# Second matmul in four 32-column array tiles where scores, pooling or weights share the session; denominators in other slots

## The chip, the cores and the metric

One core of a Trainium2 chip. The metric is the device time of one execution in microseconds (us), lower is better. The kernel before takes 597.37 us (median of 3 runs, 596.58 to 597.43).

## The reference, cut to what matters

```python
def mab(q, kv):                       # attention; C = 128, scale = 1/sqrt(C)
    a = softmax(scale * (q @ kv.T))
    return a @ kv
h = mab(inducing, x)                  # 32 inducing rows against 12480 rows of x, for 4 batches
y = mab(x, h)                         # 12480 rows of x against the 32 rows of h
hid = y @ w_in                        # 128 -> 2048
out = (max(hid, 0) + alpha * min(hid, 0)) @ w_out      # 2048 -> 128
```

The kernel never forms `y`. It multiplies `h` into `w_in` once for each batch (`hW`), so that the first large matmul of a group of 512 rows contracts over 32 rows alone; it writes the activation as relu plus a linear part; and it divides by the softmax denominator at the very end.

## The kernel before

The work of a group of 512 rows of x is cut into four *sessions* (`j` = 0 to 3), 391 in all. A session fills four PSUM banks (a fill is four matmuls of 32x128 weights, one in each 32-row tile of the array), has ScalarE (ACT) and VectorE (DVE) relu them into `gt`, and then does the 16 second matmuls of the session before it.

```python
def fill(st, g, j):                                   # cut
    for r in range(4):
        ps = bank()                                   # ring of 6 PSUM banks
        mm(ps[:, ...], st.hW[32*r : 32*r+32, j*cp + i, :], rep[32*r : 32*r+32, :t])
    ...                                               # ACT or DVE: gt[:, r] = relu(bank), by a plan

def mm2(st, g, j, gt):                                # cut: a whole group, pp = 128, nb = 4
    for r in range(4):
        for k in range(nb):
            mm(acc[:pp, k, :], gt[:, r, k0 : k0 + pp], W1[:, c, :], ...)

for b, g, j in fills:
    gt = fill(states[b], g, j)
    for fn, _ in tasks.pop((b * NG + g, j), []):
        fn()                                          # the tasks of this session
    if prev is not None:
        mm2(*prev)
    prev = (states[b], g, j, gt)
```

All else is a *task*, put into a session between its fill and its second matmuls:

```python
# scores: four matmuls with 32 columns of weights, each into its own 32 partitions of one bank
for q in range(NQ):
    mm(ps[32*q : 32*q+32, :], st.hT, st.xT[:, s, q, :])         # second scores (b_scores)
    mm(ps[32*q : 32*q+32, :], IT[:], st.xT[:, u, q, :])         # first scores of the next batch (a_scores)
# pooling (a_accum): 16 matmuls of the same form, 128 wide; weights (h_weights): four, 512 wide
# denominators (b_den): four matmuls over all 128 columns, then a reciprocal on DVE
at(g,     b_scores, 3, (320, "A", 490));   at(g + 2, b_den,   3, (130, "D", 250))
at(k,     a_load)                              # x of the next batch, 512 KB by DMA
at(k + 3, a_xpose)                             # its transpose, by DMA
at(k + 5, a_scores, 0, (320, "A", 680));   at(k + 8, a_accum, 3, (240, "D", 220))
at(K,     h_den,    3, (250, "D", 500));   at(K + 1, h_transpose, 1, ...)   # K: five groups before the end
```

The last argument tells a planner, which divides the relus between ACT and DVE, what a task costs on TensorE and on the engine that empties its bank.

The softmax here doesn't subtract the row's maximum and nothing guards it: scores larger than these inputs give would overflow.

## Time and profile before

| | before |
|---|---|
| span of the profiled run | 597.2 us |
| TensorE matmul busy | 582.9 us, 98% |
| DVE, ACT busy | 87%, 85% |
| plain session (294 of them) | 1.327 us |
| session with scores alone | 1.656 us |
| session with linear part and scores; with pooling as well | 1.872; 2.096 us |

Session times are mine, from the trace: from the first fill matmul of one session to that of the next; medians.

The page of the kernel before, busy times (time, share of the span, number of instructions) and granted clock in tenths by slice of the span:

```profile
PE 582.9 (98%) x9186; PEld 435.0 (73%) x9186; DVE 518.6 (87%) x878; ACT 507.1 (85%) x994; POOL 84.9 (14%) x170
...
PEclk9999999999999999999999999999999999999999
...
q8 instruction: 72, 1.18, 0.9%
```

The last line is the DMA queue that brings instructions: 72 packets, 1.18 MB. That is 16 KB a packet. TensorE's 18,400 instructions (loads, matmuls and 29 that wait, signal or drain) over 72 packets make 256 instructions a packet, so I read each packet as a *page* of 256 TensorE instructions.

The timeline of TensorE before, one session with scores (start, duration, what, count):

```profile
82.56 0.38 PE L94 MATMUL ring_85<-rep,hW 32*128 32x512 bf16 x1
...
82.89 0.40 PE L94 MATMUL ring_83<-xT,IT 128*32 128x512 bf16 x4
83.22 1.07 PE L94 MATMUL acc_87<-W_168,gt 128*128 128x128 bf16 x16
84.22 0.38 PE L94 MATMUL ring_84<-rep,hW 32*128 32x512 bf16 x1
```

Read the starts, since durations overlap: the second matmuls' 1.07 us end after the next fill has begun. Fill to scores takes 0.33 us, scores to second matmuls 0.33 us, second matmuls to the next fill 1.00 us. The work in these is 0.216, 0.216 and 16 x 0.056 = 0.90 us (0.216 us is what passes in this trace from the last fill of a session, at 80.475, to its linear part, at 80.691, where the tiling stays). So each change of the array's tiling (32 rows, then 32 columns, then whole) leaves about 0.105 us empty.

What a narrow second matmul would cost could be read off the pooling task, which has its form (128x32 weights, 128 wide):

```profile
81.23 0.40 PE L94 MATMUL ring_84<-xn,e1T 128*32 128x128 bf16 x16
81.56 0.23 PE L94 MATMUL acc_87<-W_168,gt 128*128 128x128 bf16 x1
```

In the trace its 16 matmuls start in groups of four at 81.232, 81.288, 81.344 and 81.400: four at once every 56 ns.

### The profile page before, as it was taken

The page shows a single profiled execution, that of the slowest core. Times are in us where ns is not written, and L with a number is a line of the kernel's source. Part 1 is how long each engine was busy: PE and PEld are TensorE (multiplying, and loading weights), DVE is VectorE, ACT ScalarE, POOL GpSimd, SP SyncE. Part 2 cuts the span into 40 slices and gives each one's busy share as a digit, 9 for nine tenths or more (in the row PEclk, how much of TensorE's full clock was granted, in tenths as well). Part 3 has the DMA queues.
Part 4 walks back from the last instruction along what each step waited for, and adds up shares of the span by engine and source line. Part 5 has one row for each costly group of instructions (what it writes and reads, how often), then busy time and mean ns, then how long its engine had stood idle before and what let it go on. Part 6 is the DMA issues. An engine that isn't in the chain of part 4 may idle for free.

```text
span 597.2 us, 21700 instructions
## 1 busy us (share of the span) xinstructions
PE 582.9 (98%) x9186; PEld 435.0 (73%) x9186; DVE 518.6 (87%) x878; ACT 507.1 (85%) x994; POOL 84.9 (14%) x170
## 2 busy tenths in 40 slices
PE   4999999999999999999999999999999999999997
PEld 3677777777777777677777777777777777777775
DVE  2588899889889998899998989988988898998995
ACT  3588888898889888888888988889888889989886
POOL 6331111010111111101011111101011101101100
PEclk9999999999999999999999999999999999999999
DMA  9644799862237669983134478986212221221211
GB/s 197 161 93 103 162 161 176 172 105 85 68 87 147 134 141 173 166 154 112 40 99 120 101 162 157 173 177 103 86 68 80 80 98 57 83 97 56 93 46 61
DMA packets 79009, 69.18 MB, mean 116 GB/s; under 512 B 53200, under 2 KB 68448, under 8 KB 78912
## 3 DMA queue, kind: packets, MB, share of 16 engines
q0 software_dynamic: 12720, 39.30, 26.4%
q1 hardware_dynamic: 66048, 27.97, 24.2%
q8 instruction: 72, 1.18, 0.9%
q10 hardware_dynamic: 144, 0.52, 0.3%
q14 instruction: 25, 0.20, 0.1%
HBM read 39.94 MB, written 28.62 MB: 115 GB/s over the span
## 4 chain that ended last, share of the span: by engine, by line
PE 58%; ACT 0%; DVE 0%; issue 0%
PE acc_88 L94 21%; PE acc_87 L94 21%; PE ring_85 L94 3%; PE ring_83 L94 3%; PE ring_84 L94 3%; PE ring_82 L94 3%; PE ring_81 L94 3%; PE ring_86 L94 3%; ACT gt L405 0%; DVE gt L407 0%; DVE ob L456 0%
## 5 line engine op out<-in xcount | busy, mean ns | idle before, releaser
L94 PEld LDWEIGHTS <-gt 128*128 128x128 bf16 x6272 | 352.4, 98 | 78.9 <-issue 75.9
L94 PE MATMUL acc_87<-W_168,gt 128*128 128x128 bf16 (+1 forms) x3136 | 209.0, 220 | 0.0
L94 PE MATMUL acc_88<-W_168,gt 128*128 128x128 bf16 (+1 forms) x3136 | 208.8, 220 | 0.0
L465 POOL DMA_DIRECT2D out_dram<-ob x99 | 53.7, 542 | 492.8 <-DVE ob L456 422.3
L405 ACT ACTIVATE gt<-ring_83 128x512 bf16<-128x512 f32 (+1 forms) x160 | 95.5, 597 | 10.9 <-ACT gt L405 5.4
L405 ACT ACTIVATE gt<-ring_81 128x512 bf16<-128x512 f32 (+1 forms) x159 | 95.0, 597 | 11.2 <-PE ring_84 L94 5.6
L94 PE MATMUL ring_82<-rep,hW 32*128 32x512 bf16 (+1 forms) x270 | 101.6, 379 | 0.0
L94 PE MATMUL ring_83<-rep,hW 32*128 32x512 bf16 (+1 forms) x270 | 101.1, 378 | 0.0
L94 PE MATMUL ring_85<-rep,hW 32*128 32x512 bf16 (+1 forms) x267 | 100.4, 379 | 0.3 <-ACT gt L405 0.3
L94 PE MATMUL ring_84<-rep,hW 32*128 32x512 bf16 (+1 forms) x266 | 99.6, 378 | 0.8 <-DVE gt L407 0.8
L94 PE MATMUL ring_86<-rep,hW 32*128 32x512 bf16 (+1 forms) x264 | 99.3, 379 | 0.0
L94 PE MATMUL ring_81<-rep,hW 32*128 32x512 bf16 (+1 forms) x263 | 98.9, 379 | 0.0
L405 ACT ACTIVATE gt<-ring_84 128x512 bf16<-128x512 f32 x147 | 88.2, 600 | 12.0 <-ACT gt L405 5.4
L405 ACT ACTIVATE gt<-ring_85 128x512 bf16<-128x512 f32 (+1 forms) x147 | 87.7, 596 | 11.8 <-PE ring_82 L94 5.3
L405 ACT ACTIVATE gt<-ring_86 128x512 bf16<-128x512 f32 (+1 forms) x143 | 85.6, 599 | 12.3 <-ACT gt L405 5.9
L405 ACT ACTIVATE gt<-ring_82 128x512 bf16<-128x512 f32 (+1 forms) x142 | 84.9, 598 | 12.1 <-PE ring_85 L94 4.4
L407 DVE TENSOR_SCALAR gt<-ring_82 128x512 bf16<-128x512 f32 (+1 forms) x123 | 84.2, 684 | 8.5 <-PE ring_84 L94 4.1
L407 DVE TENSOR_SCALAR gt<-ring_86 128x512 bf16<-128x512 f32 (+1 forms) x116 | 79.4, 684 | 12.9 <-PE ring_82 L94 8.4
L407 DVE TENSOR_SCALAR gt<-ring_84 128x512 bf16<-128x512 f32 (+1 forms) x113 | 77.1, 682 | 9.3 <-PE ring_85 L94 3.8
L407 DVE TENSOR_SCALAR gt<-ring_85 128x512 bf16<-128x512 f32 x115 | 78.9, 686 | 7.1 <-PE ring_81 L94 2.5
L407 DVE TENSOR_SCALAR gt<-ring_83 128x512 bf16<-128x512 f32 x104 | 71.4, 687 | 9.4 <-PE ring_85 L94 4.4
L407 DVE TENSOR_SCALAR gt<-ring_81 128x512 bf16<-128x512 f32 x99 | 68.0, 687 | 6.8 <-PE ring_82 L94 2.3
(321 smaller groups left out, 372.1 us busy)
## 6 DMA issues: line engine op xcount, KB each, us to landing
out_dram<-ob POOLq DMA_DIRECT2D x96, 256.0 KB, 2.8
rep<-e2d SPq DMA_DIRECT2D x92, 128.0 KB, 3.0
xn<-in_x_dram POOLq DMA_DIRECT2D x18, 512.0 KB, 6.2
xn<-in_x_dram POOLq DMA_DIRECT2D x10, 256.0 KB, 8.9
w_out_f<-in_moe_w_out_dram POOLq DMA_DIRECT2D x1, 1024.0 KB, 13.9
xs<-in_x_dram ACTq DMA_DIRECT2D x1, 512.0 KB, 4.0
xs<-in_x_dram SPq DMA_DIRECT2D x1, 512.0 KB, 5.0
w_in_b<-in_moe_w_in_dram POOLq DMA_DIRECT2D x1, 512.0 KB, 11.9
```

The lines of the kernel that those rows point to most:

```text
L94: return pin(nc.tensor.matmul(o, lhsT, rhs, start=start, stop=stop, **kw))
L405: pin(nc.scalar.activation(out=gt[:, r, :w], in_=ps[:, :w], func=RELU))
L407: pin(nc.vector.tensor_relu(gt[:, r, :w], ps[:, :w]))
L465: pin((nc.sync if last_one else nc.gpsimd).dma_start(out=dst, in_=ob[:pp, :nb, :]))
```

## The change

The intent: in a session with scores, pooling or weights, do the second matmuls in the same tiling (four 32-column tiles), so that the session changes tiling twice and not three times. Denominators, which use the whole array, leave the pooling sessions for the second session of a group.

```diff
-    def mm2(st, g, j, gt):
+    def mm2(st, g, j, gt, narrow=False):
+        step = 32 if narrow else pp
...
-                    mm(acc[:pp, k, :], gt[:, r, k0 : k0 + pp], W1[:, c, :], ...)
+                    for t in range(0, pp, step):
+                        mm(acc[t : t + step, k, :], gt[:, r, k0 + t : k0 + t + step], W1[:, c, :], ...)
...
-            at(g, b_scores, 3, (320, "A", 490))
-            at(g + 2, b_den, 3, (130, "D", 250))
+            at(g, b_scores, 3, (216, "A", 490), True)
+            at(g + 2, b_den, 1, (130, "D", 250))
-                at(k + 5, a_scores, 0, (320, "A", 680))
-                at(k + 8, a_accum, 3, (240, "D", 220))
+                at(k + 5, a_scores, 0, (216, "A", 680), True)
+                at(k + 8, a_accum, 3, (225, "D", 220), True)
-            at(K, h_den, 3, (250, "D", 500))
+            at(K + 1, h_den, 0, (250, "D", 500))
-            at(K + 1, h_weights, 3, (320, "D", 600))
+            at(K + 1, h_weights, 3, (216, "D", 600), True)
# the session's second matmuls are narrow if its last task with a cost has True
```

(Lambdas are left out of the `at` lines, here and in the edits below, which are shortened.) 60 sessions become narrow, each with 48 more weight loads and 48 more matmuls.

More of the change, by code (lines that the diff above doesn't have):

```diff
@@ L419, in mm2 @@
                     k0 = (i * nb + k) * pp
-                    mm(
-                        acc[:pp, k, :], gt[:, r, k0 : k0 + pp], W1[:, c, :],
-                        start=(j == 0 and r == 0 and i == 0 and k == 0 and not begun),
-                        stop=False, skip_group_check=True,
-                    )
+                    for t in range(0, pp, step):
+                        mm(
+                            acc[t : t + step, k, :], gt[:, r, k0 + t : k0 + t + step], W1[:, c, :],
+                            start=(j == 0 and r == 0 and i == 0 and k == 0 and not begun),
+                            stop=False, skip_group_check=True,
+                        )
         if j == NJ // cp - 1 and st.b * NG + g > 0:
@@ L605, with at @@
     tasks = {}
-    def at(slot, fn, j=1, cost=None):
-        tasks.setdefault((slot, j), []).append((fn, cost))
+    def at(slot, fn, j=1, cost=None, narrow=False):
+        tasks.setdefault((slot, j), []).append((fn, cost, narrow))
     def late_finish():
@@ L629 @@
             g = base + s * NQ - 4
-            at(g, lambda b=b, s=s: b_scores(states[b], s), 3, (320, "A", 490))
+            at(g, lambda b=b, s=s: b_scores(states[b], s), 3, (216, "A", 490), True)
             at(g + 1, lambda b=b, s=s: b_rep(states[b], s), 3)
-            at(g + 2, lambda b=b, s=s: b_den(states[b], s), 3, (130, "D", 250))
+            at(g + 2, lambda b=b, s=s: b_den(states[b], s), 1, (130, "D", 250))
         if b + 1 < B:
@@ L643 @@
                 at(k + 3, lambda n=n, u=u: a_xpose(states[n], u))
-                at(k + 5, lambda n=n, u=u: a_scores(states[n], u), 0, (320, "A", 680))
-                at(k + 8, lambda n=n, u=u: a_accum(states[n], u), 3, (240, "D", 220))
+                at(k + 5, lambda n=n, u=u: a_scores(states[n], u), 0, (216, "A", 680), True)
+                at(k + 8, lambda n=n, u=u: a_accum(states[n], u), 3, (225, "D", 220), True)
             k = base + NG - 5
             at(k, lambda n=n: h_sum(states[n]))
-            at(k, lambda n=n: h_den(states[n]), 3, (250, "D", 500))
+            at(k + 1, lambda n=n: h_den(states[n]), 0, (250, "D", 500))
             at(k + 1, lambda n=n: h_transpose(states[n]), 1, (300, "D", 250))
-            at(k + 1, lambda n=n: h_weights(states[n]), 3, (320, "D", 600))
-            at(k + 2, lambda n=n: b_scores(states[n], 0), 1, (320, "A", 490))
+            at(k + 1, lambda n=n: h_weights(states[n]), 3, (216, "D", 600), True)
+            at(k + 2, lambda n=n: b_scores(states[n], 0), 1, (216, "A", 490), True)
             at(k + 2, lambda n=n: h_linear(states[n]), 3, (80, "D", 250))
@@ L668, in make_plan @@
             lin = 240 if j == NJ // cp - 1 and lin_groups(b, g) else 0
-            costs = [c for _, c in tasks.get((b * NG + g, j), []) if c]
+            costs = [c for _, c, _ in tasks.get((b * NG + g, j), []) if c]
             idx = [(at_bank + r) % RING for r in range(4)]
@@ L733 @@
         gt = fill(states[b], g, j)
-        for fn, _ in tasks.pop((b * NG + g, j), []):
+        narrow = False
+        for fn, cost, tiled in tasks.pop((b * NG + g, j), []):
             fn()
+            narrow = tiled if cost else narrow
         if prev is not None:
-            mm2(*prev)
+            mm2(*prev, narrow)
         prev = (states[b], g, j, gt)
```

## The prediction

> **What bounds the kernel now.** TensorE. The busy table gives it 98% of 597.2 us (ACT 85%, DVE 87%); the groups show about zero idle time before its matmuls. The timeline shows the beat: a plain session is four 512-wide fills in four row tiles, then 16 second matmuls of 128x128, and takes 1.327 us. Its parts: second matmuls 56 ns apart (16 take 0.90 us), four fills side by side 0.22 us, which leaves two gaps of about 0.105 us. Each is a change of the array's tiling[...].
>
> A session with scores (four 128x32 column tiles, 512 wide) takes 1.656 us: 0.216 of streaming plus a third change, 0.11 us. With linear, scores and pooling it takes 2.096 us.
>
> **What the change does.** In 60 sessions (counted in the built order of instructions) the 16 second matmuls become 64 with 32-column weights, in the tiling that scores, pooling and weights already use.
> - Removed: one change of tiling each, scores to second matmul: 60 x 0.105 = 6.3 us.
> - Added: 96 instructions in each such session. Their array time should be the same: the pooling matmuls in this trace already have exactly this form (128x32 weights, 128 wide) and start in groups of four every 56 ns, so 16 groups take 0.90 us as before. [...]the pooling groups show no cost of it (four loads and four matmuls per 56 ns), but only for four groups in a row.
> - Denominators of 9 pooling sessions (full-array form) move to plain sessions: a pooling session with one takes 2.068 us, against 1.87 worked out without it, but a denominator costs only 0.10 us in a plain session (1.427 against 1.327). 9 x 0.095 = 0.85 us gained. Three others land before the next batch's first scores and add a change: 3 x 0.105 = 0.3 us lost.
> - The pooled-sum denominator moves to one session before the pooled transpose, which needs it by way of two DVE operations (0.16 and 0.28 us) behind the evictions: perhaps 0.2 to 0.3 us of TensorE wait, three times.
> - The eviction plan changes, DVE and ACT lose 1% of slack: up to 1 us of new stalls.
>
> All of it lies on TensorE, the critical path: 597.4 - 6.3 - 0.85 + 0.3 + about 0.9 gives 591.4 us.
>
> **Predicted: 591.3 us, 8 in 10 between 589.0 and 596.5.** Faster by over 2%: 0.02. Within 2%: 0.94. Slower by over 2%: 0.04.
>
> **What would show it.** Score sessions at 1.55 us instead of 1.656, and linear-scores-pooling sessions at 1.99 instead of 2.096; the first narrow second matmul directly behind the scores, without the 0.1 us gap; the 64 matmuls starting in groups of four, 56 ns apart. Plain sessions stay at 1.327 us.
>
> **What would make it wrong.** The narrow stream needs 128 loads and matmuls in 0.9 us, four times today's rate, and this trace has never sustained that. If instructions cannot be supplied that fast (the queue, or their fetch: pages of 256 instructions now come about every 8 us, some starting late while DMA is busy, and narrow sessions would eat one in under 3 us), groups of four will start later than 56 ns apart or in bursts with gaps called "issue", and a session may lose more than the 0.1 us gained. Then 595 to 610 us. If a change from column to row tiles costs more than from the full array, the gain vanishes too.

In the bullet on what is added, "no cost of it" means no cost of loading weights into 32-column tiles.

## More of the kernel before

Nearly all runs told of here are of the fast state. Two runs of one experiment (`e6_spread`) count as slow and are named there.

## The result, and the profile after

620.35 us median of 4 runs (616.76 to 623.46) against 597.4. The ratio is 1.038, with a 95% interval of 1.0341 to 1.0419. (A ratio here is taken over the fast runs by the program that compares them, so it is not quite the ratio of the medians quoted.) The result is correct. The profiled run took 616.76 us, with a span of 615.0.

The page after, same lines as above:

```profile
PE 586.2 (95%) x12066; PEld 440.2 (72%) x12066; DVE 515.7 (84%) x875; ACT 508.3 (83%) x997; POOL 84.9 (14%) x170
...
PEclk9999999899999999799999999999999999999999
...
q8 instruction: 94, 1.54, 1.1%
```

TensorE has holes now, the clock dips twice, and there are 22 more pages of instructions. The session itself came out as predicted. TensorE's timeline after, a session with scores:

```profile
82.10 0.40 PE L94 MATMUL ring<-rep,hW 32*128 32x512 bf16 x4
82.43 0.40 PE L94 MATMUL ring<-xT,IT 128*32 128x512 bf16 x4
82.65 1.07 PE L94 MATMUL acc<-W,gt 128*32 128x128 bf16 x64
83.65 0.40 PE L94 MATMUL ring<-rep,hW 32*128 32x512 bf16 x4
```

Scores to second matmuls is 0.22 us in place of 0.33, the 64 narrow matmuls take the same 1.00 us up to the next fill, and the session takes 1.550 us in place of 1.656. Undisturbed sessions with linear part and scores take 1.767 us, with pooling too 1.990: each 0.106 us less.

The loss is elsewhere. The same timeline shows this, 160 us later:

```profile
242.73 1.10 PE L94 MATMUL acc<-W,gt 128*32 128x128 bf16 x61
...
244.42 1.08 PE L94 MATMUL acc<-W,gt 128*32 128x128 bf16 x64
245.43 0.40 PE L94 MATMUL ring<-rep,hW 32*128 32x512 bf16 x4
245.76 0.62 PE L94 MATMUL acc<-W,gt 128*128 128x128 bf16 x8
249.37 1.03 PE L94 MATMUL acc<-W,gt 128*128 128x128 bf16 x8 [2.99 <-issue]
```

After two narrow sessions side by side, TensorE stops in the middle of a row of 16 ordinary second matmuls, after the eighth, for 3.2 us. The ninth matmul reads the third relu of the session before, and DVE and ACT had ended all four of those by 245.6 us. The profile names no engine and no DMA, just "issue": it sees nothing that the engine waits for. The waits of TensorE by releaser, the kernel after (total us, times, longest):

```profile
PE acc L94 <- issue: 13.4, 9, 3.0
```

and those of its weight loads, first before, then after:

```profile
PEld L94 <- issue: 86.8, 375, 0.9
```

```profile
PEld L94 <- issue: 96.0, 350, 3.2
```

The longest such wait was 0.9 us; it is 3.2 us now. The kernel before has no line of the first kind.

I counted TensorE's instructions up to each such stop, and put the packets of the instruction queue beside them. This is worked out from the trace after, times in us:

```
count before   page crossed   packet   packet   TensorE   TensorE
the stop       one page ago   starts   landed   goes on   stood
 3521 =13*256+193    93.54     97.60    98.60    100.14    1.32
 4033 =15*256+193   105.82    109.84   110.73    112.23    2.92
 4545 =17*256+193   120.94    121.38   122.47    123.73    0.45
 8129 =31*256+193   204.97    207.87   208.76    210.16    1.21
 9153 =35*256+193   229.12    233.41   234.35    235.88    2.76
 9665 =37*256+193   242.94    247.01   247.99    249.36    3.20
10177 =39*256+193   259.94    261.89   262.88    264.19    1.92
15297 =59*256+193   380.21    381.90   383.58    384.37    1.83
16577 =64*256+193   406.55    410.07   410.97    412.31    0.56
17601 =68*256+193   429.24    429.78   431.21    432.42    0.85
```

All ten stops stand at the same place modulo 256, which I take for the first instruction of a page, and all end 0.8 to 1.5 us after a packet of that queue has landed. I conclude that TensorE had run out of instructions. Nor is it chance: after the first 30 us every packet of the queue, in order, starts between 0.4 us before and 4.3 us after TensorE crosses into the page before the one that it would bring. (For the first stop the profile names a relu of DVE as the releaser, but that ended 0.47 us before TensorE went on.) Less the usual 56 ns, the ten sum to 16.5 us.

Two more readings. First, the time in which 256 instructions go, from page to page: 7.2 us at the least before, 2.8 us after (2.3 us up to a page's last instruction, before any stop at the next page), since a narrow session runs 144 instructions or more in 1.55 us where a plain one runs 40 in 1.33. Second, the packets are late: I take the time from TensorE's crossing of a page to the start of the packet for the next one. After, its median is 2.1 us where an x load was under way at the crossing (between its issue and its landing), 0.6 where only other DMA was, and 0.1 where none was. The kernel before has the lateness too (0.9 us beside loads, 4.2 at worst), but eight microseconds to hide it in. In the longest stop, the load had been issued 1.1 us before the page was crossed:

```profile
241.80 0.54 POOL L125 DMA_DIRECT2D xn<-in_x_dram  x1
```

The sum before a stop is: lateness (up to 4.3 us) + packet (1.0) + landing to first instruction (about 1.4), against 2.3 to 8 us of instructions in hand.

Two of the long stops cost a second time. The view of stretches after (length, busy times, then granted clock, DMA share, GB/s):

```profile
246.10:249.40 3.30, 0.31 (x7) 0.14 (x4) 1.08 (x2) 1.33 (x3) 0.54 (x1) 0.87 0.80 179
249.40:255.30 5.90, 5.90 (x52) 4.31 (x52) 2.58 (x4) 2.17 (x4) 0.00 (x0) 0.50 0.84 92
255.30:262.00 6.70, 6.70 (x188) 4.96 (x188) 5.64 (x10) 5.64 (x11) 1.08 (x2) 1.00 0.30 61
```

Behind the stop of 3.2 us the clock is granted at half, for 6.8 us in the clock records (248.5 to 255.3), and 5.9 us hold 52 matmuls, where plain sessions would do about 89 (20 in 1.327 us). The two throttled stretches (3.4 and 6.8 us) cost about 4.0 us beyond the stops, by the session times: a plain session takes 2.37 us in place of 1.327 there. They follow the stops of 2.9 and 3.2 us; the stop of 2.8 us at 235.88 is followed by none. A stop of 2.3 us in `e3_no_loads`, below, was followed by 3.4 us at half clock.

### The profile page after: what moved, and what is told of

Read it like the earlier page. It is cut to its first block, busy times and chain, and to the rows that moved or that the text cites. A ratio compares the mean times of both kernels' runs of the same rounds, so it can differ in the third digit from the quotient of the medians.

```text
span 615.0 us, 27467 instructions
## 1 busy us (share of the span) xinstructions
PE 586.2 (95%) x12066; PEld 440.2 (72%) x12066; DVE 515.7 (84%) x875; ACT 508.3 (83%) x997; POOL 84.9 (14%) x170
## 5 line engine op out<-in xcount | busy, mean ns | idle before, releaser
L405 ACT ACTIVATE gt<-ring 128x512 bf16<-128x512 f32 (+1 forms) x901 | 470.6, 598 | 87.7 <-PE ring L94 38.9
L407 DVE TENSOR_SCALAR gt<-ring 128x512 bf16<-128x512 f32 (+1 forms) x667 | 433.9, 686 | 76.2 <-PE ring L94 53.7
L94 PE MATMUL acc<-W,gt 128*128 128x128 bf16 (+1 forms) x9152 | 423.9, 220 | 14.5 <-issue 13.4
L94 PEld LDWEIGHTS <-gt 128*128 128x128 bf16 (+1 forms) x9152 | 360.9, 98 | 85.5 <-issue 79.7
L94 PE MATMUL ring<-rep,hW 32*128 32x512 bf16 (+1 forms) x1600 | 162.8, 381 | 0.5 <-ACT gt L405 0.3
L94 PEld LDWEIGHTS <-hW 32*128 32x128 bf16 x1600 | 43.0, 91 | 45.0 <-issue 2.1
L458 DVE TENSOR_TENSOR ob<-acc,rd 128x512 f32<-128x512 f32 x96 | 65.4, 682 | 1.8 <-PE acc L94 1.8
L94 PEld LDWEIGHTS <-rep 32*128 32x128 bf16 (+2 forms) x408 | 16.3, 94 | 6.3 <-issue 0.7
L94 PE MATMUL acc<-hA,rep 32*128 32x128 bf16 x392 | 19.8, 214 | 0.0
L203 ACT ACTIVATE e<-ring 128x512 bf16<-128x512 f32 x24 | 14.5, 602 | 1.9 <-PE ring L94 1.9
L309 ACT ACTIVATE e<-ring 128x512 bf16<-128x512 f32 x23 | 13.9, 604 | 0.0
```

Source lines behind the costliest of these rows:

```text
L94: return pin(nc.tensor.matmul(o, lhsT, rhs, start=start, stop=stop, **kw))
L203: pin(nc.scalar.activation(out=e1[:], in_=ps[:], func=EXP, scale=scale, accum_out=st.es[:, u : u + 1]))
L309: pin(nc.scalar.activation(out=e2[:], in_=ps[:], func=EXP, scale=scale))
L405: pin(nc.scalar.activation(out=gt[:, r, :w], in_=ps[:, :w], func=RELU))
L407: pin(nc.vector.tensor_relu(gt[:, r, :w], ps[:, :w]))
L458: pin(nc.vector.tensor_tensor(out=ob[:pp, :nb, :], in0=acc[:pp, :nb, :], in1=rbc, op=MULT))
```

## The experiments

Theory F (instruction fetch): narrow sessions use up a page before the next is there, most of all where x loads make its packet late. Rival D: the moved denominators and the new eviction plan cost the time. Rival T: narrow matmuls are slow by themselves, in loading or issue. In the tables below "page stops" are stops over 0.38 us at a page's first instruction.

### Half of the change at a time

`e1_moves_alone`: all second matmuls wide, the rest as changed.

```diff
-            mm2(*prev, narrow)
+            mm2(*prev)
```

> The change with the denominators and the plan moved, but every second matmul left 128 wide. Theory F (instruction fetch: narrow sessions use up a page of 256 TensorE instructions before the next page is there): no starvation, 597 to 599 us, 0.85 us won by the moves less about 1.3 us of waiting for the pooled transpose (three sessions of 2.06 us were seen). Rival D (the moved denominators and the new plan cost the time): 612 us or more.

Measured 600.9 us (600.78 to 601.18), ratio 1.0048 (1.0029 to 1.0068), no page stop. D is not the cause of 3.8%, but the moves, which I had taken for a gain, lose 3 us by themselves. Three pooled transposes sit in sessions of 2.06 us where it was 1.64 (1.3 us in all). And the session after most of the moved denominators runs 0.172 us long. The timeline of this kernel shows one:

```profile
64.38 3.32 DVE L407 TENSOR_SCALAR gt<-ring 128x512 bf16<-128x512 f32 x5
...
66.85 0.25 PE L94 MATMUL ring<-pick,e 128*128 128x4 bf16 x4
...
66.99 2.56 ACT L405 ACTIVATE gt<-ring 128x512 bf16<-128x512 f32 x5 [0.24 <-ACT gt L405]
67.61 0.68 DVE L458 TENSOR_TENSOR ob<-acc,rd 128x512 f32<-128x512 f32 x1
...
67.95 0.57 PE L94 MATMUL ring<-rep,hW 32*128 32x512 bf16 x4
68.21 0.25 DVE L358 RECIPROCAL rd<-ring 128x16 f32<-128x16 f32 x1
```

The four fills at 67.95 take 0.57 us and not 0.40: they start one after another as banks come free, since DVE is at its group's final multiply (`ob`) and ACT alone empties the banks of the session. In its old slot the denominator sat in a longer session (1.645 us in the trace before), with the linear part, which by my reading gave the evictions that time.

`e2_narrow_alone`: narrow second matmuls, denominators in their old slots (57 narrow sessions).

```diff
-            at(g + 2, b_den, 1, (130, "D", 250));   at(K + 1, h_den, 0, (250, "D", 500))
+            at(g + 2, b_den, 3, (130, "D", 250));   at(K,     h_den, 3, (250, "D", 500))
```

> The change with the narrow second matmuls, but the denominators in their old slots. Theory F: still starved, 612 to 622 us, stalls of 0.5 to 3 us named issue that start at every 256th instruction and end 1.3 to 1.5 us after a page lands. Rival D: close to 592 us.

Measured 611.27 us (610.24 to 614.33), ratio 1.023 (1.0194 to 1.0265): just below the expected range, and far from D's. Seven page stops, 12.0 us in all. The narrow matmuls bring the loss; the moves add to it. (I did not count an eighth stop at a page's first instruction, 1.4 us, which ended 0.2 us after a transfer of `rep` on which those matmuls wait.) The two halves lose 13.4 and 3.0 us by themselves and 23 us together; of the other 6.6 us, 4.5 us are page stops in the traces, ten in place of seven, and the rest I did not trace. The waits of TensorE by releaser, this kernel:

```profile
PE acc L94 <- issue: 10.0, 6, 2.6
```

### The DMA traffic taken away

`e3_no_loads`: the whole change, but batches 1 to 3 read batch 0's x tiles again (wrong result).

```diff
     def a_load(st, u, pieces=1):
+        if st.b:
+            st.xn[u] = loaded[u]          # the tile of batch 0
+            return
```

> The whole change, but batches 1 to 3 use the x tiles of batch 0 again, so that no x is loaded after the start (wrong result on purpose). Theory F with loads as the cause of the late fetches: fetches start within about 1 us of their page boundary, nearly all of the 19 us of stalls go, 592 to 596 us and full clock. Rival T (the narrow matmuls or their issue are slow by themselves, whatever the DMA does): about 615 us. If the fetch is simply too slow at any DMA load: 605 to 612 us.

Measured 601.82 us (601.28 to 602.44), ratio 1.006. Without the loads 18 of the 23 us of the loss are gone. I had expected 592 to 596 and that was missed, for two reasons: the moves cost their 3 us here too, and six page stops remain (5.9 us). The mean lateness of a page in the stretch with the next batch's work (30 to 445 us) fell from 1.3 to 0.6 us. The waits by releaser:

```profile
PE acc L94 <- issue: 4.4, 5, 2.1
```

`e13_narrow_quiet`: as `e2_narrow_alone`, without the loads of batches 1 to 3 and without the DMA transposes of x (wrong result).

```diff
+        if b: st.xT, st.xTr = states[0].xT, states[0].xTr
...
     def a_xpose(st, u):
+        if st.b: return
```

> Narrow second matmuls in all 57 sessions, denominators in their old slots (as e2_narrow_alone, 611 us), but batches 1 to 3 use the x tiles and the transposed x of batch 0: neither x loads nor their transposes run after the start (wrong result on purpose). Theory F: pages start within a microsecond of their boundary, stalls under 3 us in all, and the gain of the prediction is there: 591 to 595 us. If fetches starve without this traffic too: 600 us or more.

Measured 595.54 us (595.11 to 597.26), ratio 0.9976 (0.996 to 0.9992). The same order of TensorE instructions as the 611.27 us of `e2_narrow_alone`, with the DMA quiet, is faster than the kernel before. That settles T: the narrow matmuls are not slow. The kernel before was not run with the DMA quiet, but the sum closes without it: 597.4 - 57 x 0.106 + 4.2 us of page stops = 595.6. It is half a microsecond above what I expected, and five page stops remain (4.2 us): where 256 instructions go in 2.9 us from page to page, a page that starts half a microsecond late is still too late by my estimate (0.5 + 1.1 + 1.4 = 3.0; a packet took 1.1 us in the trace before, and landing to first instruction about 1.4 in the trace after). The waits by releaser:

```profile
PE acc L94 <- issue: 2.2, 4, 0.8
```

### Fewer extra instructions

`e4_two_tiles`: two 64-column tiles in place of four of 32.

```diff
-        step = 32 if narrow else pp
+        step = 64 if narrow and pp == P else pp
```

> The whole change with two 64-column tiles in place of four of 32 columns: 32 extra matmuls and loads a session become 16 pairs, a third of the extra instructions of the change, and the tiling differs from that of the scores. Theory F: score sessions back at about 1.65 us, since the change of tiling returns; few stalls, 3 us in all at most: 597 to 603 us. Rival T (narrow loads slow by themselves): sessions with narrow second matmuls longer than 1.70 us.

Measured 602.57 us (601.73 to 604.7), ratio 1.0081. No page stop; a score session takes 1.670 us. So the gain of 0.106 us needs the very tiling of the scores, and a third of the extra instructions starves nothing (256 go in 5.3 us at the least). The 602.6 us are near the moves' 600.9.

### Moving work about, to give the fetch time

`e5_loads_later`: each x load a group later. `e6_spread`: the next batch's first scores two sessions later, so that no narrow sessions are neighbours.

```diff
-                at(k, a_load)
+                at(k + 1, a_load)                                  # e5
-                at(k + 5, a_scores, 0, (216, "A", 680), True)
+                at(k + 5, a_scores, 2, (216, "A", 680), True)      # e6
```

> The whole change, but each x load issued four sessions (one group) later, so that it runs in the stretch of plain sessions rather than beside the narrow pair. Theory F: the number of instructions and of narrow sessions is the same, but page fetches that narrow sessions wait for no longer stand behind a load: stalls fall from 19 us to under 9 us, 604 to 611 us. If the timing of loads is nothing to do with it: 617 to 623 us.

> The whole change with the first scores of the next batch two sessions later, so that no two narrow sessions stand side by side; the same instructions. Theory F: the shortest time in which 256 instructions go rises from 2.8 to over 4 us, which gives a fetch 1.5 us more: stalls fall by half or more, 604 to 611 us. Rival T (each narrow session is slow by itself): 617 to 623 us.

Both missed. `e5_loads_later` took 624.59 us (621.13 to 626.68), ratio 1.0461: ten page stops (16.1 us, about as before the move), since pages crossed while a load was under way started 2.5 us late in the median, no earlier than in the change; and besides first scores that waited for their transposed x (4.2 us in its trace). `e6_spread` took 620.06 and 620.77 us in its fast runs, ratio 1.038, and 630 and 640 in two runs that count as slow, with clocks of 0.981 and 0.979: eleven page stops (17.1 us). There 256 instructions took 3.8 us at the least, about as meant, but pages beside a load started 2.8 us late in the median and 9.1 us at worst.

`e16_spread_no_loads` is `e6_spread` with the edit of `e3_no_loads`, to tell whether the spacing was of no use or was eaten by loads.

> As e6_spread (no two narrow sessions side by side, 620 to 640 us), without the x loads of batches 1 to 3 (wrong result on purpose). If spacing is of use and e6 lost it to loads: stalls nearly gone, below e3_no_loads (601.8 us, pairs side by side) by the 6 us of its stalls, 595 to 598 us. If spacing is of no use: 601 us or more, with stalls like those of e3.

Measured 600.16 us (597.25 to 600.58), ratio 1.0036: above what I expected. Its trace has three page stops (3.5 us), where `e3_no_loads` had six (5.9 us), so spacing helps once loads are gone. But it won only 1.7 us over `e3_no_loads`, as the score sessions in their new slot take 1.648 us and not 1.550. Spacing alone does not outweigh lateness beside a load. Why `e6_spread` met later pages than the change itself is left open.

### Other ways to the same gain

`e7_shared_wide`: no narrow matmul; from the kernel before, pooling moves into the session of the next first scores, so that the two share their changes of tiling, and denominators move to the third session.

```diff
-                at(k + 8, a_accum, 3, (240, "D", 220))
+                at(k + 9 if i < 5 else k + 8, a_accum, 0 if i < 5 else 3, (240, "D", 220))
-            at(g + 2, b_den, 3, (130, "D", 250))
+            at(g + 2, b_den, 2, (100, "D", 250))
```

> The kernel before, with no narrow second matmul at all: pooling moves one session on, into the session of the next scores, so that the two share their changes of tiling, and denominators stand alone in the third session of their group. No extra instruction. 15 changes of tiling less in the pooling sessions (15 x 0.105 = 1.6 us) and 9 denominators out of pooling sessions (0.85 us): 594.5 to 597 us on this chip if before is 597.5, and no fetch stalls under either theory.

Measured 598.33 us (598.15 to 598.57), ratio 1.0011: missed. The shared sessions take 1.880 us, as the sum says (1.327 + 0.107 + 0.225 + 0.216), but the 23 sessions with a denominator take 1.52 us in place of 1.43.

`e9_shared_narrow`: sharing as in `e7_shared_wide` but in the third session, where the denominators go too, and narrow matmuls in every session that holds scores, pooling or weights (51 by the count of instructions, not 45), loads and transposes moved.

> Narrow second matmuls as in the change, but in 45 sessions in place of 60 (pooling and scores share a session), none side by side in a batch, loads moved four sessions and transposes one on, pooled denominator in its old slot. Theory F: 256 instructions take over 4 us everywhere, few stalls: 590 to 596 us. Rival T: over 605 us.

Measured 598.36 us (598.0 to 599.18), ratio 1.0013 (0.9998 to 1.0028): missed. The starvation was nearly gone, one page stop of 0.6 us, and still nothing was won. The shared sessions take 1.943 us, where the sum without a change of tiling says 1.327 + 0.225 + 0.216 = 1.768, and the denominators' sessions 1.52 us again. With the tasks in sessions that have no linear part, the gain of TensorE turned into waiting for the relus to free banks; I take that from the session times and from the same pattern in `e1_moves_alone`, and did not test it by itself.

`e10_shared_wide_den3` is `e7_shared_wide` with the denominators back in the fourth session.

> As e7_shared_wide (pooling shares a session with the next scores, every second matmul 128 wide), but the denominators stay in the fourth session of their group, as in the kernel before. If their new slots cost the 0.1 us a piece that e7 showed (sessions of 1.52 us against 1.43), this gets the 2.5 us of the fewer changes of tiling: 594.5 to 596.5 us where before is 597.7. If not: 598 us again.

Measured 597.17 us (595.92 to 598.74), ratio 0.9999 (0.9978 to 1.002): missed. Denominators cost 0.10 us each again (sessions of 1.645 us with the linear part), but only six of nine leave the pooling sessions, and its trace shows single waits of 1.5 and 0.8 us away from any page boundary; the waits of the kernel before include one such of 1.2 us.

`e12_few_narrow` adds narrow second matmuls to `e10_shared_wide_den3`, but only in sessions with second scores or weights (27 by the count of instructions). `e11_few_narrow_loads` also moves loads and transposes.

```diff
 # e12, on e10:
+            at(g, b_scores, 3, (216, "A", 490), True)      # narrow; likewise h_weights and the first b_scores
 # e11, on e12:
-                at(k, a_load);      at(k + 3, a_xpose)        # in session 1
+                at(k, a_load, 3);   at(k + 3, a_xpose, 2)
```

> As e10, plus narrow second matmuls in 26 sessions only: those that hold the second scores or the weights, two groups or more apart. 26 x 0.105 = 2.7 us on top of e10; 256 instructions take over 4.5 us. Theory F: a few late pages beside loads, 0 to 3 us: 592.5 to 596 us. Rival T (narrow sessions slow by themselves): over 600 us.

> As e12_few_narrow, with each x load issued two sessions later and its transpose one later. Theory F: no load runs while a narrow session comes up, so fewer late pages than e12: 592 to 594.5 us.

Measured 595.43 us (ratio 0.9976, 0.996 to 0.9993) and 595.56 us (0.9977, 0.9961 to 0.9994). No page stop in either. The change to the loads made no difference.

`e14_few_narrow_again` is `e11_few_narrow_loads` with more rounds; `e15_more_narrow` makes nine shared sessions narrow as well.

> The same kernel as e11_few_narrow_loads, with five rounds. 594 to 596.5 us where before is 597.4, no fetch stall over 0.4 us; the ratio under 1 with its interval.

> As e14, with nine more narrow sessions, those shared by pooling and scores that stand two groups away from the narrow second scores. 9 x 0.105 = 0.95 us less than e14 if pages keep up; if they do not, a stall or two of about 1 us, and no gain over e14.

Measured 595.12 us (594.42 to 596.52), ratio 0.9959 with an interval of 0.9946 to 0.9972; and 596.48 us (595.65 to 602.84), ratio 1.0002, with one page stop of 1.7 us in its trace. So 27 narrow sessions, most of them over 20 us apart, win 0.2% to 0.4% (two series of the same kernel), the best of all with the right result; nine more seem to lose it again, though the intervals just touch. TensorE in `e14_few_narrow_again`, a narrow session, then a wide one in which pooling and scores share:

```profile
81.24 0.40 PE L94 MATMUL ring<-xT,hT 128*32 128x512 bf16 x4
81.47 1.07 PE L94 MATMUL acc<-W,gt 128*32 128x128 bf16 x64
82.46 0.40 PE L94 MATMUL ring<-rep,hW 32*128 32x512 bf16 x4
82.79 0.41 PE L94 MATMUL ring<-xn,e1T 128*32 128x128 bf16 x16
83.02 0.39 PE L94 MATMUL ring<-xT,IT 128*32 128x512 bf16 x4
83.34 1.07 PE L94 MATMUL acc<-W,gt 128*128 128x128 bf16 x16
```

The whole picture of fetch, all from the traces:

| run | extra TensorE instructions | shortest time of 256 | page stops, sum | median us |
|---|---|---|---|---|
| before | 0 | 7.2 us | 0 | 597.4 |
| after | 5760 | 2.8 | 10, 16.5 us | 620.35 |
| `e2_narrow_alone` | 5472 | 2.7 | 7, 12.0 us | 611.27 |
| `e3_no_loads` | 5760 | 2.9 | 6, 5.9 us | 601.82 |
| `e13_narrow_quiet` | 5472 | 2.9 | 5, 4.2 us | 595.54 |
| `e4_two_tiles` | 1920 | 5.3 | 0 | 602.57 |
| `e9_shared_narrow` | 4896 | 4.0 | 1, 0.6 us | 598.36 |
| `e14_few_narrow_again` | 2592 | 4.1 | 0 | 595.12 |

## Why the prediction was wrong

- **What bounds the kernel, and the price of a change of tiling:** right. 0.106 us went from every undisturbed narrow session, and `e4_two_tiles`, with 1.670 us a score session, shows that it goes only if the tiling is the same.
- **"Added: 96 instructions in each such session. Their array time should be the same":** this is the step that failed. The array time is the same: 64 narrow matmuls in the 1.00 us of 16 wide ones. The step costed the added instructions by array time alone. But instructions are a supply of their own, and it ran dry: 16.5 us of page stops in the profiled run and about 4.0 us more at half clock behind the two longest. With the 3 us of the moves, less the 60 x 0.106 us gained, this makes 17 of the 19 us by which the profiled run was longer; about 2 us I did not itemize. The prediction had the figures: pages every 8 us, "some starting late while DMA is busy", one page eaten "in under 3 us". It named this as what would make it wrong, sized it at 595 to 610 us, under what was measured, and gave a loss of over 2% a chance of 0.04. A sum was possible: the trace before shows a packet 4.2 us late at the worst and 1.1 us long, so over 5 us against 3.
- **Denominators, "0.85 us gained", and "up to 1 us of new stalls":** wrong in sign. The moves alone cost 3 us (`e1_moves_alone`). I costed the slot by TensorE time alone; the second session of a group is where DVE does the group's final multiply (0.68 us in `e1_moves_alone`).
- **Pooled transpose, "perhaps 0.2 to 0.3 us" three times:** right in kind, 0.42 us each.
- **Loading narrow weights, "but only for four groups in a row":** no cost was seen for 16 groups of four in a row either: they start 55 to 56 ns apart in the trace after.
- **Still open:** what in the DMA makes an instruction packet wait for a load. The runs show the lateness (2.1 us in the median beside a load, 0.1 with no DMA under way) and that without the loads 18 of the 23 us of the loss go and the mean lateness falls from 1.3 to 0.6 us, not by which queue or rule.

## What to carry to other kernels

Splitting a matmul into tiles that run side by side cost no array time here (1.00 us for 64 as for 16), but each tile needs its own load and matmul: divide the page (256 instructions here) by the new rate of instructions, and see that it stays well over the time in which a page can arrive beside the heaviest DMA (here up to 4.3 us of lateness in the change and 9.1 in `e6_spread`, about 1.0 for the packet and about 1.4 to the first instruction; a kernel in which 256 went in 5.3 us at the least had no page stop, those with 2.7 to 2.9 us had five to ten, and at 3.7 to 4.1 us it went either way: no stop in `e14_few_narrow_again`, three in `e16_spread_no_loads`, eleven in `e6_spread`). Look for stops named "issue" in the middle of a row of like instructions, and count instructions modulo the page (all ten stops here stood at one place modulo 256) before blaming an engine. A slot that is free on the busiest engine may be the tightest on the engines that empty its banks (here the session after most of the moved denominators ran 0.172 us long); cost a move on both.
